# A planned order with new lengths for the vector engines' operations, a lock between two of them, and the last tile's copy in two halves

## The chip, the core and the metric

The kernel runs on one core of a Trainium2 chip. The metric is the device time of one execution in microseconds (us). PE is TensorE with its matmuls, PEld its weight loads, DVE is VectorE, ACT is ScalarE, POOL is GpSimd and SP is SyncE, which here only issues DMAs.

## What is computed

Eight batches of eight heads, each with 512 local and 32 global tokens of 64 values. The local queries see the global keys and a band of local keys, the global queries see all keys. Then every token (512 values over the heads) goes through a feed-forward layer of width 2048.

```python
def _attn_ref(q_l, k_l, v_l, q_g, k_g, v_g):
    ...
    window = 32
    scale = 1.0 / np.sqrt(D)
    k_all = np.concatenate([k_g, k_l], axis=2)
    v_all = np.concatenate([v_g, v_l], axis=2)
    s_g = scale * np.matmul(q_g, k_all.transpose(0, 1, 3, 2))
    out_g = np.matmul(sm(s_g), v_all)
    s_ll = scale * np.matmul(q_l, k_l.transpose(0, 1, 3, 2))
    pos = np.arange(Sl)
    mask = np.abs(pos[:, None] - pos[None, :]) <= window
    s_ll = np.where(mask, s_ll, -1000000000.0)
    s_lg = scale * np.matmul(q_l, k_g.transpose(0, 1, 3, 2))
    s_l = np.concatenate([s_lg, s_ll], axis=-1)
    a_l = sm(s_l)
    out_l = np.matmul(a_l, np.concatenate([v_g, v_l], axis=2))
    return np.concatenate([out_g, out_l], axis=2).astype(np.float32)

def _moe_ref(x, w_in, w_out):
    h = x @ w_in
    g = h - np.tanh(h)
    return (g @ w_out).astype(np.float32)
```

All inputs and the output are 32-bit floats; `sm` is a softmax over the last axis.

## The kernel before

**Precision.** Each operand of the feed-forward layer is split into a high part (rounded to the matmul's 32-bit type, fp32r) and a low part (the rest), and each product is made as three matmuls: high by high, low by high, high by low. So a chunk of tokens has, beside its matmuls, a cast for the high part and a subtract for the low part of everything that is made on the chip.

**Stages.** The attention of the first pairs of heads uses plain 128 x 128 transposes on PE (L547, L1176), scores L656, peak L1104 and reciprocals (L671, L672) on DVE, exponentials L1111 on ACT and the normalization L1117 on POOL, which writes `prob` or `t`; the products are L814. Later pairs use DVE's 32 x 32 stream transposes (L697, L709, L1152), band scores L730, peak L1132 (DVE), exponential L1137 (ACT), inverse L1141 and L1142 (DVE), normalization L1146 (POOL) and products L830. The global queries have scores L1030 (first pairs) and L972 (later, in halves), and turns of their probabilities L786, L788, L793, L795 on DVE. L853, L856 and L858 on DVE take the products apart into the low part of the token matrix and the sum for the global rows (`xg`).

**The feed-forward layer** runs in chunks, one for each batch of 512 local tokens (chunks of 16 steps of the hidden width, 128 columns each) and a last one for the 256 global tokens. A step is: L1219, 12 matmuls into one PSUM buffer (a `bank`) that give h; L1227, the tanh on ACT into `t`; L1230, t = h - tanh(h) on DVE; a cast of `t` to the high part of `gates` (L364, the copy helper's line, on ACT); L1236, `gates`' low part as a subtract; and L1282, which multiplies the gates by `w_out` into four accumulators (12 matmuls of 512 columns for each step). The rows of the output are copied out of PSUM (L364 `wraw<-bank`) and sent by L1312.

**Weights.** They arrive in 32 pieces beside the first 120 us or so: L418 loads a piece into `wraw` or `first_q`, L429 (ACT), L433 and L438 (DVE) bring it to the form `sq`, L364 casts the high part (`w_in_hi`, `w_out_hi`), and L444 makes the low part, on POOL or DVE.

**What sets the order.** `Order` is a list planner that runs when the program is built. Every operation is given to it by `add(engine and length, function, due, ...)` with its reads, writes, reserved names and PSUM buffers. The planner simulates five engines (T for PE, A, D, P, S) with these lengths and takes, again and again, the operation that can start first, with `KD * due` added to the start; where two engines are possible (`either`, `subtract`) each has a penalty out of the table `CFG`. A due time is made of the step and an offset of that table. An operation with `lock=True` on DVE, and each one on POOL, holds a common line "L", so that the plan never lets the two overlap. `filler` (L1509) puts up to six dummy matmuls on PE where the plan shows it a gap of over 0.6 us in the first 72 us. The instructions then stand on each engine's queue in the plan's order, and each waits at its queue's head until what it needs is done.

## Time and profile before

| | |
|---|---|
| median of three runs | 911.08 us (910.80 to 911.83) |
| the profiled execution | 911.43 us |
| its span, first to last instruction | 909.5 us |
| mean granted clock of PE, as a share | 0.995 |
| busy PE / DVE / ACT / POOL | 893.2 / 499.2 / 363.5 / 347.4 us |
| gates' subtract L1236, all 136 on POOL | 175.3 us |
| L1230 on DVE, 136 | 93.6 us |
| copies `wraw<-bank` 128x512: DVE 21, ACT 13 | 13.9 and 7.2 us |

The span is the time between the first and the last instruction of the profiled execution; the execution itself is 1.9 us longer. Times in the trace are counted from the span's start. A matmul's busy time is modelled at its end, since matmuls are pipelined: a group of L1282 shows 0.39 us each, while they follow each other more closely. An entry of the timeline may join several instructions of one line (its count is the x at its end), and the bracket gives the time in which the engine stood still before it and the operation that released it.

### The profile page before, as it was taken

The numbers are of one execution on the slowest core, as the hardware profiler recorded it, in microseconds if no ns is written. First come the engines' busy times: TensorE is split into PE (matmuls) and PEld (weight loads), VectorE is DVE, ScalarE is ACT, GpSimd is POOL, SyncE is SP. The second block draws the span as 40 slices with busy tenths as digits, with TensorE's granted clock in tenths as the row PEclk, the third lists the DMA queues.
The fourth block names the chain that finished last, engine by engine and source line by source line (L and its number), as shares of the span: only waits on it lengthen the run. The fifth ranks groups of instructions, "written<-read, shape, count | busy, mean of one in ns | idle before, by whom it ended". The sixth has DMA issues, their size and how long they took to land.

```text
span 909.5 us, 23414 instructions
## 1 busy us (share of the span) xinstructions
PE 893.2 (98%) x9101; PEld 719.4 (79%) x9101; DVE 499.2 (55%) x1829; ACT 363.5 (40%) x1024; POOL 347.4 (38%) x506
## 2 busy tenths in 40 slices
PE   8999899999999999999999999999999999999998
PEld 5678678788878878788878788787888788888896
DVE  6898878836648364746557374746566461211211
ACT  5886555523334343333344343433333331222221
POOL 5576675423333333333334333333333331222221
PEclk9999999999999999999999999999999999999999
DMA  9776674755546344645545443644555321100100
GB/s 203 189 189 184 189 185 110 181 117 115 119 97 163 79 99 103 157 111 120 120 117 142 100 100 87 161 105 110 117 137 133 94 66 30 47 1 1 45 2 23
DMA packets 286958, 101.13 MB, mean 111 GB/s; under 512 B 254848, under 2 KB 277376, under 8 KB 286848
## 3 DMA queue, kind: packets, MB, share of 16 engines
q1 hardware_dynamic: 284800, 98.53, 44.4%
q8 instruction: 71, 1.16, 0.5%
q10 hardware_dynamic: 2048, 1.11, 0.4%
q14 instruction: 39, 0.32, 0.1%
HBM read 76.01 MB, written 21.50 MB: 107 GB/s over the span
## 4 chain that ended last, share of the span: by engine, by line
PE 88%; DVE 5%; DMA 2%; ACT 1%; SPq 1%; POOL 1%; issue 1%; ACTq 0%; DVEq 0%
PE bank L1219 39%; PE bank L1282 39%; PE bank L830 4%; PE bank L730 3%; DVE sq L438 1%; PE bank L814 1%; PE bank L972 1%; DMA first_q<-in_moe_w_out_dram 1%; PE bank L656 1%; PE bank L1030 1%; SPq L686 1%; DMA raw<-in_q_l_dram 0%; DMA wraw<-in_moe_w_in_dram 0%; DMA turned<-in_v_l_dram 0%; DVE t L1230 0%
## 5 line engine op out<-in xcount | busy, mean ns | idle before, releaser
L1236 POOL TENSOR_TENSOR gates<-t,gates 128x512 fp32r<-128x512 f32 x136 | 175.3, 1289 | 390.4 <-PE bank L1282 294.1
L1282 PE MATMUL bank<-w_out_hi,gates 128*128 128x512 f32 x1088 | 296.8, 392 | 2.4 <-ACT gates L364 1.5
L1282 PEld LDWEIGHTS bank<-w_out_hi,gates 128*128 128x128 f32 x1088 | 202.7, 188 | 47.1 <-ACT gates L364 2.2
L1230 DVE TENSOR_TENSOR t<-bank,t 128x512 f32<-128x512 f32 x136 | 93.6, 689 | 234.9 <-ACT t L1227 233.8
L1227 ACT ACTIVATE t<-bank 128x512 f32<-128x512 f32 x136 | 81.2, 597 | 273.2 <-PE bank L1219 270.0
L1282 PE MATMUL bank<-w_out_lo,gates 128*128 128x512 f32 x544 | 150.7, 391 | 0.0
L364 ACT CAST gates<-t 128x512 fp32r<-128x512 f32 x136 | 84.2, 619 | 133.6 <-PE bank L1282 83.6
L1219 PE MATMUL bank<-x_hi,w_in_hi 128*128 128x512 f32 x432 | 124.6, 404 | 0.0
L1282 PEld LDWEIGHTS bank<-w_out_lo,gates 128*128 128x128 f32 x544 | 102.0, 188 | 21.7 <-issue 0.2
L1219 PE MATMUL bank<-x_lo,w_in_hi 128*128 128x512 f32 x432 | 118.9, 391 | 0.0
L1219 PE MATMUL bank<-x_hi,w_in_lo 128*128 128x512 f32 x432 | 118.4, 390 | 0.0
L1146 POOL TENSOR_SCALAR prob<-prob,stats 128x128 f32<-128x128 f32 x224 | 82.8, 387 | 57.1 <-DVE stats L1142 56.6
L1137 ACT ACTIVATE prob<-prob,stats 128x128 f32<-128x128 f32 x224 | 86.9, 390 | 34.2 <-DVE stats L1132 34.2
L1219 PEld LDWEIGHTS bank<-x_lo,w_in_hi 128*128 128x128 f32 x432 | 81.4, 189 | 17.9 <-issue 0.2
L1219 PEld LDWEIGHTS bank<-x_hi,w_in_lo 128*128 128x128 f32 x432 | 81.0, 188 | 17.8
L1219 PEld LDWEIGHTS bank<-x_hi,w_in_hi 128*128 128x128 f32 x432 | 78.0, 189 | 20.5 <-issue 4.0
L793 DVE STREAM_TRANSPOSE turned<-pg 32x96 f32<-32x96 f32 x288 | 77.7, 270 | 4.3
L1132 DVE CUSTOM_DVE_ANT_0 prob<-bank,band 128x128 f32<-128x128 f32 x224 | 50.6, 283 | 38.4 <-PE bank L730 37.8
L1152 DVE STREAM_TRANSPOSE sq<-prob 128x512 f32<-128x512 f32 x50 | 35.3, 710 | 13.3 <-POOL prob L1146 11.6
L1137 ACT ACTIVATION_READ_ACCUMULATOR prob<-prob,stats 128x1 f32 x224 | 42.1, 188 | 0.0
L830 PEld LDWEIGHTS bank<-turned 128*32 128x32 f32 x3072 | 33.1, 111 | 8.5 <-DVE stats L1142 6.7
L853 DVE TENSOR_TENSOR x_lo<-bank,x_hi 128x256 fp32r<-128x256 f32 x56 | 23.4, 419 | 29.1 <-ACT x_hi L364 26.6
(161 smaller groups left out, 916.7 us busy)
## 6 DMA issues: line engine op xcount, KB each, us to landing
moved<-sq SPq DMA_DIRECT2D x24, 512.0 KB, 3.9
turned<-in_v_l_dram SPq DMA_DIRECT2D x23, 512.0 KB, 5.5
turned<-in_v_l_dram SPq DMA_DIRECT2D x32, 256.0 KB, 3.2
out_dram<-wraw SPq DMA_DIRECT2D x32, 256.0 KB, 2.4
rawkq<-in_q_l_dram SPq DMA_DIRECT2D x112, 64.0 KB, 2.3
rawkq<-in_k_l_dram SPq DMA_DIRECT2D x112, 64.0 KB, 2.3
turned<-moved SPq DMA_DIRECT2D x48, 128.0 KB, 2.7
turned<-moved SPq DMA_DIRECT2D x96, 64.0 KB, 2.3
```

What stands on the lines that cost most here:

```text
L364: (nc.scalar.copy if e == "A" else eng[e].tensor_copy)(dst, src)
L793: nc.vector.transpose(win_g[G * g:G * g + G, a.two, 3 * x:3 * x + 3], view(pgh[r, a.two, G * (j + x):G * (j + x) + 1], [(3 * G, 3), (1, G)]))
L830: m = nc.tensor.matmul(y, win_v[:, NW * a.two + w, G * d:G * d + G], x, start=n == 0, stop=n == 7, skip_group_check=True)
L1132: nc.vector.tensor_tensor_reduce(out=x[:, t], in0=self.scores[:, t], in1=bands[0 if t == 0 else 2 if t == NT - 1 else 1], scale=-0.125, sc ...
L1137: nc.scalar.activation(x[:, t], x[:, t], AF.Exp, bias=self.st[:, t:t + 1], scale=-1.0, accum_out=self.st[:, 4 + t:5 + t])
L1146: nc.gpsimd.tensor_scalar(x[:, t], x[:, t], self.st[:, 8 + t:9 + t], 1.0, op0=ALU.mult, op1=ALU.mult)
L1152: nc.vector.transpose(z[:, :, self.two].rearrange("p n t c -> p t n c"), x[:, :, k * n * G:(k + 1) * n * G].rearrange("p t (n c) -> p t n ...
L1219: nc.tensor.matmul(self.h[s][:, j * n:(j + 1) * n], w[:, cc, f * P:(f + 1) * P], self.x()[xi](cc)[:, :n], start=part == 0 and cc == 0 and ...
L1227: nc.scalar.activation(tt_[q], self.h[s], AF.Tanh)
L1230: nc.vector.tensor_sub(tt_[q], self.h.pop(s), tt_[q])
L1236: eng[e].tensor_sub(gg[q][1], tt_[q].rearrange("p (k c) -> p k c", k=4), f32(gg[q][0]))
L1282: nc.tensor.matmul(self.acc[tt], g[:, j * nt + tt], low_out(f) if wi else w_out_hi[:, f], start=s == 0 and k == 1, stop=last and k == 3 * ...
```

## The change

The table `CFG` of offsets and penalties is new from end to end. Lengths in the calls of `add` are set anew, mostly by some hundredths of a microsecond, some by up to half a microsecond. The two operations `inverse` of the local pairs (the reciprocals of L672, and L1141 with L1142) get `lock=True`, so that the plan keeps them apart from POOL's. The copies of global keys cost less on POOL in the plan. And the last row tile of the last chunk is copied in two halves, one by DVE and one by ACT; its DMAs wait for both. Lines behind L1315 are 10 later in the changed kernel, those from L1509 on 11.

```diff
-    CFG = dict(a_g=-0.566, a_kg=24.4216, a_ph=0.3207, a_qs=43.4596, a_w=-0.4573, a_wn=-0.6947, a_xg=108.5443, d_g=87.2943, d_kg=23.5203,
...
+    CFG = dict(a_g=-2.1233, a_kg=-0.0964, a_ph=-0.2641, a_qs=5.2608, a_w=-5.4882, a_wn=-5.0581, a_xg=150, d_g=3.6283, d_kg=1.9778, d_ph=50.4226,
...
-        p = [("P", 0.17 + n * 0.00192, CFG["p_" + kind])] if "p_" + kind in CFG else []
+        p = [("P", 0.17 + n * (0.0009 if kind == "kg" else 0.00192), CFG["p_" + kind])] if "p_" + kind in CFG else []
...
-            add(("A", 0.655), rebias, due, r=keys, w=keys + [("up", u)])
-            add(("D", 0.42), low, due, r=keys, w=keys, lock=True)
+            add(("A", 0.67), rebias, due, r=keys, w=keys + [("up", u)])
+            add(("D", 0.48), low, due, r=keys, w=keys, lock=True)
...
-            add(("D", 0.37), inverse, n[0][1] - 0.5, r=[x[3] for x in n], w=[x[2] for x in n])
+            add(("D", 0.37), inverse, n[0][1] - 0.5, r=[x[3] for x in n], w=[x[2] for x in n], lock=True)
...
-                add(("D", 1.35 if self.j >= OWN else 1.75), turn, self.due(self.C["o_tg"]), r=["pg0"], w=[f"hg{a.two}"])
+                add(("D", 1.65 if self.j >= OWN else 1.6), turn, self.due(self.C["o_tg"]), r=["pg0"], w=[f"hg{a.two}"])
...
-            add(("D", 1.5), peak, due(1), r=[sg, ("mask", 1), "of"], w=all_ + [st], free=[(sg, 1), (sh, 1)])
-            add(("A", 0.95), exp, due(1.5), r=[st], w=all_)
-            add(("D", 0.65), inverse, due(2), r=["pg0"], w=[st])
-            add(("P", 1.45), norm, due(2.5), r=[st], w=all_)
+            add(("D", 2.05), peak, due(1), r=[sg, ("mask", 1), "of"], w=all_ + [st], free=[(sg, 1), (sh, 1)])
+            add(("A", 1.15), exp, due(1.5), r=[st], w=all_)
+            add(("D", 1.1), inverse, due(2), r=["pg0"], w=[st])
+            add(("P", 1.25), norm, due(2.5), r=[st], w=all_)
...
-            add(("D", 1.16), peak, d(1), r=[s] + [("band", j) for j in range(3)], w=[p, st], free=[(s, 1)])
-            add(("A", 1.6), exp, d(1.5), r=[st], w=[p])
-            add(("D", 0.33), inverse, d(2), r=[p], w=[st])
-            add(("P", 1.5), norm, d(2.5), r=[st], w=[p])
+            add(("D", 0.95), peak, d(1), r=[s] + [("band", j) for j in range(3)], w=[p, st], free=[(s, 1)])
+            add(("A", 1.64), exp, d(1.5), r=[st], w=[p])
+            add(("D", 0.38), inverse, d(2), r=[p], w=[st], lock=True)
+            add(("P", 1.45), norm, d(2.5), r=[st], w=[p])
...
-                    add(either(512, "y", True), out_copy, due + 0.5, r=[acc], w=[key], free=[(acc, 1)])
+                    if self.final and tt == nt - 1:
+                        def half(lo):
+                            def fn(e, _, tt=tt, key=key):
+                                copy(e, wraw[key[1]][:, lo:lo + DM // 2], self.acc[tt][:, lo:lo + DM // 2])
+                            return fn
+
+                        add(("D", 0.42), half(DM // 2), due + 0.5, r=[acc], w=[key + ("b",)], res=[key], free=[(acc, 2)])
+                        add(("A", 0.37), half(0), due + 0.5, r=[acc], w=[key], free=[(acc, 2)])
+                    else:
+                        add(either(512, "y", True), out_copy, due + 0.5, r=[acc], w=[key], free=[(acc, 1)])
...
-                    add(("S", 0.6 * k), out_dma(runs[:k]), due + 0.5, r=[key], w=[("out", self.name, tt)], xfer=0.78)
+                    parts = [key, key + ("b",)] if self.final and tt == nt - 1 else [key]
+                    add(("S", 0.45 * k), out_dma(runs[:k]), due + 0.5, r=parts, w=[("out", self.name, tt)], xfer=0.78)
...
+    chunks[-1].final = True
```

**What it does to the instructions.** On PE the matmuls are the same in number but for the dummies, 13 before and 21 now. Of the 136 subtracts L1236, DVE had none and now has 101; POOL had all and now has 35. Of the 32 subtracts L444, DVE had none and now has nine. The copies `wraw<-bank` were 21 on DVE and 13 on ACT; now DVE has the one half, and ACT all others. Thirty copies of global keys go from POOL to ACT, six copies of a bank into the first keys from DVE to ACT, and four casts of `xg` from ACT to DVE. In the steady state PE changes between its kinds of work as often as before (27 groups of L730, 24 of L830, 12 of L972).

DVE's queue at the first gates of the feed-forward layer (`t_66` and `t_67` are the two buffers for the tanh, `bank_` numbers are PSUM buffers); before:

```order
L433 TENSOR_SCALAR first_q<-first_q 128x512
L438 SCALAR_TENSOR_TENSOR sq<-first_q 128x512
L1230 TENSOR_TENSOR t_67<-bank_103,t_67 128x512
L1152 STREAM_TRANSPOSE x_hi1b<-prob_92 128x4x2x32
L1152 STREAM_TRANSPOSE x_lo1b<-prob_92 128x4x2x32
L1141 TENSOR_SCALAR stats<-stats 128x4
L1142 RECIPROCAL stats<-stats 128x4
L1230 TENSOR_TENSOR t_66<-bank_105,t_66 128x512
```

and now:

```order
L444 TENSOR_TENSOR w_in_lo<-sq,w_in_hi 128x4x128
L433 TENSOR_SCALAR first_q<-first_q 128x512
L438 SCALAR_TENSOR_TENSOR sq<-first_q 128x512
L1230 TENSOR_TENSOR t_67<-bank_102,t_67 128x512
L1230 TENSOR_TENSOR t_66<-bank_103,t_66 128x512
L697 STREAM_TRANSPOSE kw<-rawkq 128x8x64
```

The transposes L1152 now stand further ahead, L1141 and L1142 further behind, and the two L1230 follow each other; a subtract L444 has come to DVE just ahead.

PE's queue around the products L814 that stood at 99 us (`bank_98` to `bank_101` are the four buffers that the hidden steps and the attention share); before:

```order
L1219 MATMUL bank_99<-x_hi_75,w_in_hi 128x512 x4
L1219 MATMUL bank_99<-x_lo_76,w_in_hi 128x512 x4
L1219 MATMUL bank_99<-x_hi_75,w_in_lo 128x512 x4
L1219 MATMUL bank_100<-x_hi_75,w_in_hi 128x512 x4
L1219 MATMUL bank_100<-x_lo_76,w_in_hi 128x512 x4
L1219 MATMUL bank_100<-x_hi_75,w_in_lo 128x512 x4
L814 MATMUL bank_98<-turned 64x160 x4
L814 MATMUL bank_98<-turned 64x128 x4
L814 MATMUL bank_99<-turned 64x160 x4
L814 MATMUL bank_99<-turned 64x128 x2
L814 MATMUL bank_99<-turned 64x160 x2
```

and now:

```order
L1219 MATMUL bank_98<-x_hi_75,w_in_hi 128x512 x4
L1219 MATMUL bank_98<-x_lo_76,w_in_hi 128x512 x4
L1219 MATMUL bank_98<-x_hi_75,w_in_lo 128x512 x4
L814 MATMUL bank_99<-turned 64x160 x4
L814 MATMUL bank_99<-turned 64x128 x4
L814 MATMUL bank_100<-turned 64x160 x4
L814 MATMUL bank_100<-turned 64x128 x2
L814 MATMUL bank_100<-turned 64x160 x2
L1219 MATMUL bank_101<-x_hi_75,w_in_hi 128x512 x4
L1219 MATMUL bank_101<-x_lo_76,w_in_hi 128x512 x4
L1219 MATMUL bank_101<-x_hi_75,w_in_lo 128x512 x4
```

The products take other buffers, `bank_99` and `bank_100` in place of `bank_98` and `bank_99`, and one of the two groups of L1219 ahead of them now stands behind them.

ACT's queue at the end of the program (`bank_104` and `bank_105` are accumulators of the last chunk's two row tiles, `wraw_64` the buffers for the output); before:

```order
L1227 ACTIVATE t_67<-bank_100 128x512
L364 CAST gates<-t_67 128x4x128
L1227 ACTIVATE t_66<-bank_98 128x512
L364 CAST gates<-t_66 128x4x128
L1312 DMA out_dram<-wraw_64 32x512 x4
L1541 UNCONDITIONAL_BRANCH
```

and now:

```order
L1227 ACTIVATE t_66<-bank_101 128x512
L364 CAST gates<-t_66 128x4x128
L364 COPY wraw_64<-bank_105 128x512
L1312 DMA out_dram<-wraw_64 32x512 x2
L364 COPY wraw_64<-bank_104 128x256
L1312 DMA out_dram<-wraw_64 32x512 x2
L1552 UNCONDITIONAL_BRANCH
```

Before, both copies stood on DVE and ACT had the four DMAs alone; now ACT copies the first tile, issues two DMAs, copies its half of the second and issues the other two, while DVE's last row is the other half.

## Rows read from the trace of the kernel before

**Rows 1.** The page's first part: busy us, share of the span, instructions.

```profile
PE 893.2 (98%) x9101; PEld 719.4 (79%) x9101; DVE 499.2 (55%) x1829; ACT 363.5 (40%) x1024; POOL 347.4 (38%) x506
```

**Rows 2.** Busy us (instructions) of PE, PEld, DVE, ACT, POOL; clock, DMA share, GB/s.

```profile
0.00:25.00 25.00, 20.61 (x115) 14.12 (x117) 16.16 (x78) 15.36 (x47) 14.29 (x36) 0.93 0.93 217
...
75.00:100.00 25.00, 23.45 (x120) 19.19 (x121) 19.67 (x48) 14.40 (x31) 16.91 (x16) 1.00 0.70 183
...
100.00:125.00 25.00, 23.00 (x162) 17.42 (x159) 21.95 (x65) 15.28 (x39) 17.68 (x22) 0.93 0.65 184
...
875.00:900.00 25.00, 25.00 (x157) 22.49 (x156) 3.46 (x5) 5.78 (x10) 5.17 (x4) 1.00 0.00 1
```

**Rows 3.** Timeline of PE: start, busy, line, names, count [idle before <-releaser].

```profile
14.94 0.97 PE L1176 MATMUL bank<-idr,prob 128*128 128x128 f32 x4 [0.63 <-POOL prob L1117]
...
41.41 0.44 PE L1176 MATMUL bank<-idr,t 128*128 128x128 f32 x2 [0.15 <-POOL t L1117]
```

**Rows 4.** Timeline, all engines, at the first gates.

```profile
61.01 1.28 POOL L444 TENSOR_TENSOR w_out_lo<-sq,w_out_hi 128x512 fp32r<-128x512 f32 x1
...
61.16 0.59 ACT L1227 ACTIVATE t<-bank 128x512 f32<-128x512 f32 x1
...
61.20 1.12 DVE L1141 TENSOR_SCALAR stats<-stats 128x4 f32<-128x4 f32 x1
...
61.30 0.97 PE L1282 MATMUL bank<-w_out_hi,gates 128*128 128x512 f32 x3 [0.69 <-ACT gates L364]
...
63.16 0.50 PE L1282 MATMUL bank<-w_out_hi,gates 128*128 128x512 f32 x1 [0.89 <-DVE t L1230]
```

**Rows 5.** Timeline, all engines, around 99 us.

```profile
98.68 0.69 DVE L1230 TENSOR_TENSOR t<-bank,t 128x512 f32<-128x512 f32 x1 [1.18 <-ACT t L1227]
...
99.42 0.98 PE L814 MATMUL bank<-turned 128*64 128x160 f32 x12 [1.55 <-DVE t L1230]
```

**Rows 6.** Timeline around 106 us, then the clock of three stretches, columns as in 2.

```profile
105.88 1.28 DVE L433 TENSOR_SCALAR first_q<-first_q 128x512 int32<-128x512 int32 x1
...
108.70 1.58 PE L730 MATMUL bank<-kw,hi 64*32 64x128 f32 x62 [2.00 <-DVE xg L856]
...
108.70:110.00 1.30, 1.30 (x62) 1.12 (x62) 1.26 (x7) 1.05 (x2) 1.28 (x2) 0.69 0.78 170
...
110.00:112.00 2.00, 2.00 (x15) 1.49 (x5) 1.80 (x11) 1.36 (x7) 1.24 (x2) 0.50 0.64 223
...
112.00:113.00 1.00, 1.00 (x4) 0.76 (x3) 1.00 (x8) 0.85 (x4) 0.00 (x0) 0.69 0.03 4
```

**Rows 7.** Timeline around 175 us, of two windows.

```profile
171.83 1.68 DVE L793 STREAM_TRANSPOSE turned<-pg 32x96 f32<-32x96 f32 x6
...
175.15 0.73 PE L1282 MATMUL bank<-w_out_hi,gates 128*128 128x512 f32 x2 [0.79 <-ACT gates L364]
```

**Rows 8.** Groups of instructions: names, shapes xcount | busy us, mean ns | idle before.

```profile
L1236 POOL TENSOR_TENSOR gates<-t,gates 128x512 fp32r<-128x512 f32 x136 | 175.3, 1289 | 390.4 <-PE bank L1282 294.1
...
L1230 DVE TENSOR_TENSOR t<-bank,t 128x512 f32<-128x512 f32 x136 | 93.6, 689 | 234.9 <-ACT t L1227 233.8
...
L1132 DVE CUSTOM_DVE_ANT_0 prob<-bank,band 128x128 f32<-128x128 f32 x224 | 50.6, 283 | 38.4 <-PE bank L730 37.8
...
L1141 DVE TENSOR_SCALAR stats<-stats 128x4 f32<-128x4 f32 x56 | 13.2, 235 | 4.4 <-ACT prob L1137 4.4
...
L364 ACT COPY wraw<-bank 128x512 f32<-128x512 f32 x13 | 7.2, 584 | 4.3 <-DMA out_dram<-wraw 2.7 <-PE bank L1282 1.6
```

**Rows 9.** Timeline of the last matmuls, the last copy and ACT's issues.

```profile
904.78 0.40 PE L1282 MATMUL bank<-w_out_lo,gates 128*128 128x512 f32 x1
...
904.79 2.23 ACTq L1312 DMA_DIRECT2D out_dram<-wraw  x4
...
905.02 0.39 PE L1282 MATMUL bank<-w_out_hi,gates 128*128 128x512 f32 x1
...
905.44 0.69 DVE L364 COPY wraw<-bank 128x512 f32<-128x512 f32 x1 [0.68 <-PE bank L1282]
```

More of the change, by code (lines that the diff above doesn't have):

```diff
@@ L596, in add_transpose @@
             add(("T", 0.42), mm, due, r=[f"pg{u}"], w=[tg], res=["hg0", "hg1"], alloc=[(tg, self.tag)], rows=0.5, mode=1)
-            add([("A", 0.6, 0.0), ("D", 0.65, CFG.get("d_tg", PEN))], store, due + 0.3, r=[tg], w=["hg0", "hg1"], free=[(tg, 1)])
+            add([("A", 0.48, 0.0), ("D", 0.65, CFG.get("d_tg", PEN))], store, due + 0.3, r=[tg], w=["hg0", "hg1"], free=[(tg, 1)])
         def add_values(self):
@@ L872, in add_products @@
                 add(either(256, "ph", True), high(p), due + 0.5, r=[o[p]], w=[k + (0,) for k in x[p]])
-                add(("D", 0.55 if new else 0.65), rest(p), due + 1, r=[o[p]] + [k + (0,) for k in x[p]], w=[k + (1,) for k in x[p]] + xg_, free=[(o[p], 1)])
+                add(("D", 0.55 if new else 0.73), rest(p), due + 1, r=[o[p]] + [k + (0,) for k in x[p]], w=[k + (1,) for k in x[p]] + xg_, free=[(o[p], 1)])
     def add_globals(b):
```

32 lines of the change are left out of this document (16 added, 16 removed).

## The prediction

> **What bounds the kernel now.** I read the busy times first. PE works 893.2 of the 909.5 us of the span [rows 1], so a change of order can take away no more than the 16.3 us in which PE stands still, plus what the clock loses. Next the stretches of 25 us: PE is busy 20.61 in the first, 23.45 in the fourth, 23.00 in the fifth and 25.00 of 25 in one near the end [rows 2]; behind 175.15 us no entry of PE's timeline carries an idle time. So all that this change can win lies in the first 175 us and in the tail; the 730 us between can only lose. Then those entries, from left to right.
>
> The start: seven waits for POOL's normalized probabilities (L1117, L1050), the first of 0.63 and the last of 0.15, together 4.13 us [rows 3].
>
> The first gates: L1282, which needs the gates of the FFN's first two steps, waits 0.69 for ACT's cast and then 0.89 for the second L1230 (DVE, h - tanh h) [rows 4]. Ahead of that L1230 stood L1141, an operation on 4 columns, for 1.12 us beside a POOL subtract (L444) of 1.28; over the kernel L1141 takes 0.235 in the mean [rows 4, 8].
>
> At 99.42 a product L814 waits 1.55 for an L1230 that began only at 98.68 [rows 5]. At 108.70 the band scores L730 wait 2.00 for L856, which stood on DVE behind the weight operation L433 of 1.28 [rows 6]. After it the granted clock is 0.69, 0.50 (1.2 of 2.4 GHz) and 0.69 for 1.30, 2.00 and 1.00 us [rows 6]: 0.31 x 1.30 + 0.50 x 2.00 + 0.31 x 1.00 = 1.71 us lost, while it is 1.00 in the fourth stretch [rows 2]. At 175.15 L1282 waits 0.79 for a cast whose L1230 stood behind groups of six L793, 1.68 us each [rows 7].
>
> The tail: the last matmul starts at 905.02, 0.24 after the one before it, and the last tile's copy takes 0.69 from 905.44 [rows 9].
>
> **The change part by part.** The new durations and the lock enter only the plan; no instruction gets cheaper by them. PE has the same matmuls in both orders but for the dummies (13 before, 21 after), so I cost the places.
>
> First gates. In the new order DVE's two L1230 stand back to back and L1141 behind them, and ACT runs both L1227 before the first cast. So the 0.89 is gone, the first cast may come up to one L1227 (0.59) later [rows 4], partly inside the dummies ahead of it: I take -0.7. Ends: -1.58 (both waits gone) and 0.
>
> At 99 us. Before, L814 took two buffers, one of which an L1219 had filled 24 matmuls earlier and which waited for its L1230. Now it takes two that are long free, and an L1219 group stands on each side. The 1.55 goes, unless L814's other operands are late. Ends: -1.55 and 0.
>
> At 106 us. Before, 24 L1282 stood between L814 and the L730 that reuses its buffer, at 0.24 each [rows 9] 5.8 us of cover, in which DVE lost 1.28 to one operation. Now 12 L1219, 20 L1282, 12 L1219 and 4 L1282 come before the next user of those buffers, 48 x 0.24 = 11.5 us. The 2.00 goes and the clock's 1.71 with it. Ends: -3.71 and 0.
>
> At 175 us. Two groups of six L793 still stand ahead of the L1230. Ends: -0.79 and 0.
>
> Together 0.7 + 1.55 + 3.71 + 0.79 = 6.75 us if all goes (7.63 by the ends). What is late next? The weight pieces are prepared up to about 115 us, each with an L433 and an L438 that exclude POOL's work; between 100 and 125 us DVE is busy 21.95 and POOL 17.68 of 25 us [rows 2]. One blocked operation at a queue's head was enough for each of the waits above, and where one goes the queue behind it shows the next. I let half come back elsewhere, for want of a row that says which: **-3.4**, ends 0 and -7.6.
>
> The gates' subtract. 101 of the 136 L1236 move from POOL to DVE. A subtract of this size takes 1.289 on POOL; on DVE the nearest row is L1230 with 0.689 [rows 8]: 70 us on an engine that is busy 499 of 909 [rows 1]. The step's chain (L1227, L1230, cast, L1236) comes to 0.59 + 0.69 + 0.6 + 0.69 = 2.6 us with the cast at about the ACT copy's time [rows 4, 8], and PE has 48 matmuls or so between a step's last L1219 and its first L1282 in the steady state, 11.5 us. I cost it at nothing. That cover fails only where DVE's queue is late, which is rival (d).
>
> L1236 has both operands in SBUF, and the rows show that a DVE operation beside POOL's can be stretched: L1141 by 0.9 us [rows 4, 8]. The Trainium skill (SBUF — State Buffer, Who interferes with whom) has a rule that speaks against this move: a DVE instruction with two SBUF inputs and a GpSimd instruction that reads SBUF share a pair of ports, one of the two waits until the other is done, and a DVE instruction with one SBUF input (L1230, whose other input is in PSUM) doesn't. By it each moved L1236 can be late by what POOL runs at the time; no row of this trace has L1236 on DVE.
>
> The start. Six copies of bank into the first keys and four of first_g move to ACT, and DVE has two transposes and two L444 more but six copies less ahead of its first L1230. ACT's six, at 0.584 at most [rows 8], are 3.5 us if each lies on the path; the eight more dummies (8 x 0.24 = 1.9 us) lie inside such waits. On the other side half of the 4.13 us of POOL's waits may go, since POOL gives up copies and subtracts: -2.1. That the new plan has more gaps that draw dummies speaks for the later end: I take **+0.5**, ends -2.1 and +3.5.
>
> The tail. Before, ACT's four issues lie in 904.79 to 907.02 [rows 9], two of them after the copy's end at 906.13, so 0.45 each. Now ACT copies the first tile (0.584 [rows 8], to about 904.7), issues two and then copies its half: start 905.6, 0.29 to 0.58 long, end 905.9 to 906.2 in place of 906.13. **-0.1**, ends -0.25 and +0.1.
>
> Sum: -3.4 + 0.5 - 0.1 = -3.0. The profiled execution took 911.43, which is 0.35 over the median of 911.08: the sum gives 908.4 on it and 908.1 on the median.
>
> **The rivals.**
> (a) All late waits go and the start keeps its time: -6.75 - 0.1, **904.2**. For it: each of the three large waits hangs on one place in two queues, and the new order changes each. Against: the same three engines feed the same stretch.
> (b) The start gets later by ACT's copies and eats the gain: -3.4 + 3.5 - 0.1, **911.1**. For it: 21 dummies in place of 13. Against: POOL, for which PE waited there, gets lighter.
> (c) The order doesn't matter here: the weights' arrival and blocked operations set the stretch from 60 to 125 us whatever stands where, **911.0**. For it: DVE's 21.95 of 25 us [rows 2]. Against: the buffers of L814 really differ.
> (d) Slower, by new waits in the gapless part. In the new order the global halves' scores L972 follow 12 L1282 after the L730 whose buffers they take, at five sites: 12 x 0.24 = 2.9 us. In that time DVE must do eight L1132, 50.6/224 = 0.226 each [rows 8], and an L1230: 1.8 + 0.69 = 2.5. With an L1236 among them it is 3.2; with that one held up by a POOL operation of 1.29 [rows 8] it is 4.5, and PE waits 1.6. Five sites are 8.0 us, 908.1 + 8.0 = **916.1**. Four make it slower by more than a measurement's bound (908.1 + 6.4 = 914.5), two only take the gain. For it: there is no slack once an L1236 stands between, and the rule above, by which it comes out so where POOL is at work. Against: POOL, busy 347 of 909 us with the subtracts [rows 1], has lost most of them.
>
> **How the numbers follow.** Forecast (half of the waits) 0.38, (a) 0.23, (b) 0.15, (c) 0.09, (d) 0.15. A measurement of this kernel can tell about 0.2%, 1.8 us, from no change: faster is below 909.3, slower above 912.9. The forecast's own spread is some 2 us to each side, so 0.33 of its 0.38 are faster; with (a) and the milder 0.06 of (b), 0.62. Same: 0.05 of the forecast, 0.08 of (b) and (c), 0.22. Slower: (d) and the rest of (b), 0.16. The range leaves out the start's gain on top of (a), and most of (d): 904.0 to 912.5.
>
> **What would show it.** Right: no idle entry of PE over 1 us between 63 us and the tail, a granted clock of 1.00 from 100 to 125 us, the second L1230 of the first gates 0.7 after the first, L814 and L730 near 100 us with no DVE releaser, and 101 L1236 on DVE near 0.69 each. Rival (a): PE's idle times from 63 to 176 us add to less than 1 us. Rival (b): the first L1282 later than 61.30 by 2 us or more. Rival (c): they still add to 4 or more. Rival (d): L972 or L730 idle behind 175 us with DVE as releaser, and L1236 on DVE well over 0.69 in the mean. The forecast is wrong in kind if PE idles in the part that was gapless.

## The result: 6 us slower

| | before | changed |
|---|---|---|
| median | 911.28 us | 917.39 us |
| lowest to highest of four | 910.80 to 911.83 | 915.89 to 919.13 |
| the profiled execution / its span | 911.43 / 909.5 us | 916.99 / 915.2 us |
| start of the first L1282 | 61.30 | 63.46 |
| from there to the end of the span | 848.2 us | 851.7 us |
| idle entries of PE: up to 60 us / from there to 180 us / behind | 5.81 / 5.92 / 0 us | 6.51 / 4.68 / 3.87 us |
| L1219 behind the same matmuls | 176.19 | 175.93 |
| L1282 behind the same matmuls, near 234 us | 233.99 | 233.78 |
| L1282 behind the same matmuls, near 900 us | 896.98 | 902.52 |
| last matmul's start to the end, by the unrounded spans | 4.53 us | 4.65 us |

The ratio is 1.0068 with the interval 1.0048 to 1.0087. 917.4 lies beyond the range (904.0 to 912.5) and on the other side. (The 6.51 holds a wait of 1.75 us at 57.78, which belongs to the first gates.)

"Behind the same matmuls" means: counted line by line and without the dummies, PE has by then done the same matmuls in both kernels. So the two starts can be compared, though the orders differ. The lines near 234 and 900 us, first of the kernel before, then of the changed one:

```profile
233.99 1.07 PE L1282 MATMUL bank<-w_out_hi,gates 128*128 128x512 f32 x4
...
896.98 1.09 PE L1282 MATMUL bank<-w_out_hi,gates 128*128 128x512 f32 x4
```

```profile
233.78 1.07 PE L1282 MATMUL bank<-w_out_hi,gates 128*128 128x512 f32 x4
...
902.52 1.09 PE L1282 MATMUL bank<-w_out_hi,gates 128*128 128x512 f32 x4
```

The changed kernel is 2.2 us later at the first L1282, level again at 176 us and at 234, and 5.5 later near 900 us. So its loss lies behind 234 us: 668.74 us in place of 662.99, which is 5.75 more. The time in front of it varies from execution to execution: four profiled executions of this same order (this one and three of the runs below) start that L1219 at 175.33 to 177.64.

The page of the changed kernel, in the order of [rows 1] and [rows 8]: busy times and three groups.

```profile
span 915.2 us, 23456 instructions
...
PE 895.0 (98%) x9109; PEld 720.6 (79%) x9109; DVE 550.6 (60%) x1916; ACT 386.2 (42%) x1078; POOL 204.3 (22%) x366
...
L1230 DVE TENSOR_TENSOR t<-bank,t 128x512 f32<-128x512 f32 x136 | 92.9, 684 | 173.1 <-ACT t L1227 172.7
...
L1236 DVE TENSOR_TENSOR gates<-t,gates 128x512 fp32r<-128x512 f32 x101 | 70.5, 698 | 100.0 <-PE bank L1282 91.2
...
L1236 POOL TENSOR_TENSOR gates<-t,gates 128x512 fp32r<-128x512 f32 x35 | 46.1, 1319 | 47.2 <-PE bank L1282 25.7
```

PE is busy 1.8 us longer, which is the length of the eight more dummies: 12 L1282 follow one another in 2.72 us (228.33 to 231.05), 0.2265 each. DVE is up by 51 us, POOL down by 143. The moved L1236 take 698 ns each on DVE, near L1230's 684.

The first gates, timeline of ACT, PE and DVE, and then an entry of SP's queue (answer to [rows 4]):

```profile
56.80 0.67 ACT L429 ACTIVATE wraw<-wraw 128x512 f32<-128x512 f32 x1 [1.68 <-DMA wraw<-in_moe_w_in_dram]
...
57.78 0.49 PE L1245 MATMUL bank<-x_hi,w_in_hi 128*128 128x512 f32 x1 [1.75 <-ACT x_hi L364]
...
59.67 0.62 ACT L364 CAST w_in_hi<-sq 128x512 fp32r<-128x512 f32 x1 [0.40 <-DVE sq L438]
...
60.20 0.67 ACT L429 ACTIVATE first_q<-first_q 128x512 f32<-128x512 f32 x1
...
60.78 1.05 ACT L1227 ACTIVATE t<-bank 128x512 f32<-128x512 f32 x2
...
62.07 1.28 DVE L1230 TENSOR_TENSOR t<-bank,t 128x512 f32<-128x512 f32 x2
...
63.46 1.30 PE L1282 MATMUL bank<-w_out_hi,gates 128*128 128x512 f32 x4 [2.43 <-ACT gates L364]
...
52.16 0.43 SPq L418 DMA_DIRECT2D wraw<-in_moe_w_in_dram  x1
```

The two L1230 run back to back (1.28 for both), L1141 is gone from between them, and the wait of 0.89 with it. But all of it stands later. On ACT an L429 stood 1.68 at the queue's head for a piece of w_in, whose load L418 was issued at 52.16 between two sets of raw loads L686 (49.06 and 52.69), and the cast of x_hi behind it made PE wait 1.75. Then ACT runs a cast and an L429 of weight pieces before the two L1227, and L1282 waits 2.43: 4.18 in the place of 1.58.

The stretch behind it, by windows (columns as in [rows 2]), and two of the five waits from 64 to 176 us that stand where 1.55, 2.00 and 0.79 stood ([rows 5 to 7]):

```profile
64.00:66.00 2.00, 2.00 (x7) 1.52 (x6) 1.74 (x6) 1.94 (x7) 2.00 (x3) 0.61 0.79 247
...
66.00:68.00 2.00, 2.00 (x7) 1.56 (x6) 1.96 (x4) 0.70 (x4) 0.84 (x1) 0.54 0.59 89
...
100.00:125.00 25.00, 24.65 (x168) 19.05 (x168) 19.82 (x61) 15.90 (x40) 17.32 (x20) 1.00 0.64 176
```

```profile
92.30 2.23 PE L814 MATMUL bank<-turned 128*64 128x160 f32 x30 [0.59 <-DVE turned L786]
...
165.83 1.70 PE L814 MATMUL bank<-turned 96*64 96x128 f32 x24 [0.66 <-DMA turned<-sq]
```

The five waits add to 0.59 + 0.35 + 0.40 + 0.25 + 0.66 = 2.25 us in place of 4.34. The clock is whole between 100 and 125 us; but behind the waits at the first gates it loses 0.39 x 2 + 0.46 x 2 = 1.70 us between 64 and 68, as much as behind the wait at 108.70 before. From the first L1282 to the L1219 at 176 us it is 114.9 us before and 112.5 now: the smaller waits win back what the first gates lost.

Behind 176 us, where the kernel before had no idle entry, PE waits at 11 places, always an L830 for the last L795 of the turn. One of them, with DVE's and POOL's queues ahead of it:

```profile
225.71 0.42 DVE L982 CUSTOM_DVE_ANT_0 pg<-bank,mask 128x256 f32<-128x256 f32 x1
...
226.87 0.68 DVE L977 COPY stats<-stats 32x2 f32<-32x2 f32 x4
...
228.96 1.37 DVE L977 COPY stats<-stats 32x2 f32<-32x2 f32 x4
...
231.36 1.30 DVE L1152 STREAM_TRANSPOSE sq<-prob 128x512 f32<-128x512 f32 x2
...
232.58 0.60 DVE L895 STREAM_TRANSPOSE qgt<-qgt 64x128 f32<-64x128 f32 x2
...
235.12 1.68 DVE L793 STREAM_TRANSPOSE turned<-pg 32x96 f32<-32x96 f32 x6
...
236.82 0.20 DVE L795 STREAM_TRANSPOSE turned<-pg 32x32 f32<-32x32 f32 x1
...
228.20 2.80 POOL L1146 TENSOR_SCALAR prob<-prob,stats 128x128 f32<-128x128 f32 x8 [21.21 <-DVE stats L1141]
...
231.03 1.00 POOL L1003 TENSOR_SCALAR pg<-pg,stats 128x288 f32<-128x288 f32 x2
...
237.07 1.56 PE L830 MATMUL bank<-turned 128*32 128x64 f32 x128 [0.42 <-DVE turned L795]
```

DVE has no gap from the peak L982 at 225.71 to the end of the turn at 237.02: 11.3 us. PE has 48 matmuls of L1219 and L1282 between L972 and this L830, 48 x 0.2265 = 10.9 us (48 or 44 at the other places). In the kernel before it has 72 (56 at one place), and the turn's last L795 ends 2.5 to 8.8 us ahead of each of these L830. The plan's lengths for the halves' inverse (1.1) and the turn (1.65) are short of what stands here: 1.37 for four L977 and 0.47 more for L997 and L998, and 1.68 + 0.20.

The end of the program (answer to [rows 9]):

```profile
910.56 0.39 PE L1282 MATMUL bank<-w_out_hi,gates 128*128 128x512 f32 x1
...
910.99 0.42 DVE L364 COPY wraw<-bank 128x256 f32<-128x256 f32 x1 [4.74 <-PE bank L1282]
...
911.45 0.37 ACT L364 COPY wraw<-bank 128x256 f32<-128x256 f32 x1 [1.25 <-DVE wraw L364]
```

By the profile ACT's half was released by DVE's half: the halves run one behind the other and end 1.26 after the last matmul's start; the whole copy ended 1.11 after it.

### The profile page after: what moved, and what is told of

The parts are those of the page before. It is cut to its first block, busy times and chain, and to the rows that moved or that the text cites. A ratio compares the mean times of both kernels' runs of the same rounds, so it can differ in the third digit from the quotient of the medians.

```text
span 915.2 us, 23456 instructions
## 1 busy us (share of the span) xinstructions
PE 895.0 (98%) x9109; PEld 720.6 (79%) x9109; DVE 550.6 (60%) x1916; ACT 386.2 (42%) x1078; POOL 204.3 (22%) x366
## 3 DMA queue, kind: packets, MB, share of 16 engines
q10 hardware_dynamic: 2048, 1.11, 0.5%
## 4 chain that ended last, share of the span: by engine, by line
PE 74%; DVE 16%; ACT 4%; DMA 2%; SPq 2%; issue 2%; POOL 0%; ACTq 0%; DVEq 0%; POOLq 0%
PE bank L1282 33%; PE bank L1219 31%; DVE turned L793 4%; PE bank L830 4%; PE bank L730 3%; DVE stats L977 2%; DVE t L1230 2%; SPq L752 1%; DVE sq L1152 1%; PE bank L972 1%; DVE sq L438 1%; DVE pg L982 1%; PE bank L1245 1%; ACT turned L364 1%; DVE turned L795 1%
## 5 line engine op out<-in xcount | busy, mean ns | idle before, releaser
L1282 PE MATMUL bank<-w_out_hi,gates 128*128 128x512 f32 x1088 | 299.3, 395 | 2.8 <-ACT gates L364 2.8
L1282 PEld LDWEIGHTS bank<-w_out_hi,gates 128*128 128x128 f32 x1088 | 200.8, 188 | 50.8 <-issue 5.0
L1230 DVE TENSOR_TENSOR t<-bank,t 128x512 f32<-128x512 f32 x136 | 92.9, 684 | 173.1 <-ACT t L1227 172.7
L1146 POOL TENSOR_SCALAR prob<-prob,stats 128x128 f32<-128x128 f32 x224 | 91.1, 425 | 457.6 <-DVE stats L1142 264.0
L1227 ACT ACTIVATE t<-bank 128x512 f32<-128x512 f32 x136 | 80.8, 596 | 234.1 <-PE bank L1219 233.7
L1282 PE MATMUL bank<-w_out_lo,gates 128*128 128x512 f32 x544 | 151.7, 393 | 0.1
L1236 DVE TENSOR_TENSOR gates<-t,gates 128x512 fp32r<-128x512 f32 x101 | 70.5, 698 | 100.0 <-PE bank L1282 91.2
L1219 PE MATMUL bank<-x_hi,w_in_hi 128*128 128x512 f32 x432 | 120.5, 395 | 0.0
L1282 PEld LDWEIGHTS bank<-w_out_lo,gates 128*128 128x128 f32 x544 | 102.5, 188 | 22.4 <-issue 0.3
L1219 PE MATMUL bank<-x_hi,w_in_lo 128*128 128x512 f32 x432 | 118.6, 390 | 0.0
L1219 PE MATMUL bank<-x_lo,w_in_hi 128*128 128x512 f32 x432 | 118.3, 390 | 0.0
L1219 PEld LDWEIGHTS bank<-x_lo,w_in_hi 128*128 128x128 f32 x432 | 81.0, 188 | 17.3 <-issue 0.2
L1219 PEld LDWEIGHTS bank<-x_hi,w_in_lo 128*128 128x128 f32 x432 | 80.6, 188 | 17.6 <-issue 0.2
L1219 PEld LDWEIGHTS bank<-x_hi,w_in_hi 128*128 128x128 f32 x432 | 79.6, 188 | 17.6 <-issue 0.6
L793 DVE STREAM_TRANSPOSE turned<-pg 32x96 f32<-32x96 f32 x288 | 77.5, 269 | 5.6
L1236 POOL TENSOR_TENSOR gates<-t,gates 128x512 fp32r<-128x512 f32 x35 | 46.1, 1319 | 47.2 <-PE bank L1282 25.7
L1152 DVE STREAM_TRANSPOSE sq<-prob 128x512 f32<-128x512 f32 x50 | 34.6, 703 | 33.5 <-POOL prob L1146 32.1
L830 PEld LDWEIGHTS bank<-turned 128*32 128x32 f32 x3072 | 33.4, 111 | 13.1 <-DVE turned L795 8.5
```

The lines of the kernel that those rows point to most:

```text
L793: nc.vector.transpose(win_g[G * g:G * g + G, a.two, 3 * x:3 * x + 3], view(pgh[r, a.two, G * (j + x):G * (j + x) + 1], [(3 * G, 3), (1, G)]))
L830: m = nc.tensor.matmul(y, win_v[:, NW * a.two + w, G * d:G * d + G], x, start=n == 0, stop=n == 7, skip_group_check=True)
L1146: nc.gpsimd.tensor_scalar(x[:, t], x[:, t], self.st[:, 8 + t:9 + t], 1.0, op0=ALU.mult, op1=ALU.mult)
L1152: nc.vector.transpose(z[:, :, self.two].rearrange("p n t c -> p t n c"), x[:, :, k * n * G:(k + 1) * n * G].rearrange("p t (n c) -> p t n ...
L1219: nc.tensor.matmul(self.h[s][:, j * n:(j + 1) * n], w[:, cc, f * P:(f + 1) * P], self.x()[xi](cc)[:, :n], start=part == 0 and cc == 0 and ...
L1227: nc.scalar.activation(tt_[q], self.h[s], AF.Tanh)
```

## The experiments

In most of them the plan is made as it stands and single operations are then moved in the finished list, past operations on which they don't depend; everything else keeps its place. The kernel before measured 910.8 to 911.6 beside each of them.

### The turn and L830

```diff
+    for j in range(10, 32, 2):
+        i = next(i for i, v in enumerate(out) if _name(v).endswith("mm_windows") and ("o0", "pair", j) in v[2].args)
+        k = next(k for k in range(i + 1, len(out)) if out[k][3] == "T")
+        _hoist(out, k, i)
```

> The changed kernel with its order kept, but at the 11 places from 237 to 745 us where L830 waited for the turn L795 (0.20 to 0.57 us each, 3.87 together), the L1219 or L1282 group behind L830 (4 matmuls, 0.9 us) is put ahead of it. Theory A (the loss is these waits): they vanish, and at 0.05 to 0.1 more than the idle time for each, 4.5 to 5.5 us go: 917.4 becomes 912 to 913. Theory B (the loss is in the first 175 us, where the first gates wait 1.75 and 2.43): the time stays above 915. Theory C (DVE is too full): the waits come back at the next place where PE needs DVE.

Measured 914.70 (ratio to the kernel before 1.0035, 1.0022 to 1.0048). The 11 waits are gone, as theory A says, though 914.70 is later than its 912 to 913; one wait of 0.54 at 650 us is new.

```diff
...
+        for k in turns:                      # the two turns of the pair, behind the norm
+            _hoist(out, k, at)
+            at += 1
```

> The changed kernel, with DVE's queue alone altered: at the same 11 places the turn (L793, L795) stands directly behind the normalization's place in the plan, ahead of one or two L1152 (0.65 each) and L895 (0.60). Theory A1 (the turn is late for what stands ahead of it on DVE): at 237 us it can start at 232.03, when POOL's L1003 ends, in place of 233.22, so the waits vanish and 912 to 913 comes out as in the first run. Theory A2 (POOL's norm sets it): the waits shrink by less than half, 915 or more.

Measured 913.70 (1.0031, 1.0018 to 1.0045). The place at 237 us, timeline:

```profile
236.07 0.20 DVE L795 STREAM_TRANSPOSE turned<-pg 32x32 f32<-32x32 f32 x1
...
237.11 1.57 PE L830 MATMUL bank<-turned 128*32 128x64 f32 x128
```

The turn ends 0.84 us ahead of L830 (0.1 at places with 44 matmuls), with the same matmuls in between as in the changed kernel; one wait of 0.57 at 649 us is new. Of the 6.1 us, 2.7 to 3.7 go with the waits, less than expected. In the profiled executions the stretch from the L1282 near 234 us to that near 900 us takes 664.26 and 664.39 us in these two runs, 668.74 in the changed kernel and 662.99 in the kernel before: the 11 waits cost 4.4 of the 5.75 us, more than their 3.87 of idle time, and 1.3 to 1.4 are left, about 1 of them around the new wait. A1 holds, A2 falls.

```diff
...
+        if v[0] > 180 and v[3] == "D" and _name(v).endswith("Chunk.add_hidden.rest"):
+            out[i] = (*v[:3], "P")
```

> The changed kernel with its order kept, but from 180 us on all gates' subtracts L1236 (98) go back from DVE to POOL, at their places in the order. Theory C (the moved subtracts fill DVE): near 225 us an L1236 waited 0.43 for PE and took 0.69 just ahead of the peak L982; without it the turn is up to 1.1 us earlier and the 11 waits of L830 vanish: 912 to 913. Theory A (the place of L830 in the order alone): the waits stay, 916 to 918.

Measured 919.04 (1.0093, 1.0076 to 1.0111): the waits didn't vanish, they grew to 6.84 us in 11 entries.

```profile
231.62 1.29 POOL L1236 TENSOR_TENSOR gates<-t,gates 128x512 fp32r<-128x512 f32 x1 [0.23 <-ACT gates L364]
...
234.63 1.77 DVE L793 STREAM_TRANSPOSE turned<-pg 32x96 f32<-32x96 f32 x6
...
236.69 1.56 PE L830 MATMUL bank<-turned 128*32 128x64 f32 x128 [0.65 <-DVE turned L795]
```

A POOL subtract of 1.29 now lies beside the turn, and six L793 take 1.77 in place of 1.68. From 234 to 900 us it takes 671.05, which is 2.3 us more than the changed kernel. So theory C falls: the moved subtracts don't make the waits, and in this order they are a gain.

```diff
...
+        if v[0] > 180 and v[3] == "P" and _name(v).endswith("Chunk.add_hidden.rest"):
+            out[i] = (*v[:3], "D")
```

> The kernel before, its order kept, but all gates' subtracts L1236 from 180 us on are made by DVE in place of POOL, at the same places in the order. The prediction's step (the move costs nothing in the steady state, since PE has 40 matmuls and more between a step's L1219 and its L1282): 911 within 1 us, and no idle entry of PE behind 180 us. Rival by the port rule (an L1236 on DVE is held up by POOL's norms): L1236 well over 0.69 in the mean, and PE waits: 913 or more.

Measured 911.60 (1.0010, 1.0000 to 1.0021), and no idle entry behind 180 us; from 234 to 900 us it takes 663.17, 0.2 more than the kernel before. The group of DVE's subtracts:

```profile
L1236 DVE TENSOR_TENSOR gates<-t,gates 128x512 fp32r<-128x512 f32 x116 | 80.1, 690 | 88.5 <-PE bank L1282 71.4 <-ACT gates L364 15.1 <-ACT turned L364 1.4
```

### Offsets and lengths

`g1_offsets_only` is the kernel before with the new table, `g2_lengths_only` the changed kernel with the old table.

> The kernel before with the new table of offsets alone (old lengths, no lock, old tail). In its order 40 matmuls of L1219 and L1282 stand between the scores L972 and the L830 that needs their turn; in the changed kernel it is 44 or 48, in the kernel before 72. 40 x 0.2265 = 9.1 us against the 11.3 us that DVE needed from the peak L982 to the end of the turn (225.7 to 237.0 in the changed kernel). Theory A (the offsets put L830 too near): waits of about 2 us at each of 10 or 11 places, 20 us and more: 930 or later. Theory D (the new lengths or the lock did it): no such waits, 909 to 913.

Measured 944.20 (1.0364). The first of these waits:

```profile
243.09 2.57 PE L830 MATMUL bank<-turned 128*32 128x64 f32 x128 [2.74 <-DVE turned L795]
```

11 such entries, 0.64 to 2.98 each and 18.9 us together, about as expected from 40 matmuls. The first L1282 starts at 69.59, which is 8.3 us more.

> The changed kernel with the old table of offsets (new lengths, lock and tail). 72 matmuls between L972 and L830, as in the kernel before. Theory A: no waits of L830 for the turn; the time is that of the kernel before but for the first 175 us and the tail, 909 to 913. Theory D: L830 waits and 914 or more.

Measured 933.87 (1.0251). No L830 waits for its turn: that half of theory A holds. From 234 to 900 us it takes 663.12, as in the kernel before. The time was missed by 20 us, because the start falls apart with these lengths and the old offsets (the first L1282 starts at 78.41); the longest wait in front of it:

```profile
55.22 0.80 PE L587 MATMUL bank<-idr,pg 64*128 64x64 f32 x5 [4.46 <-POOL pg L1050]
```

So the two halves of the change belong together; neither table is good with the other's lengths. The short distance from L972 to L830 comes with the new table.

```diff
-                add(("D", 1.65 if self.j >= OWN else 1.6), turn, self.due(self.C["o_tg"]), r=["pg0"], w=[f"hg{a.two}"])
+                add(("D", 1.9 if self.j >= OWN else 1.9), turn, self.due(self.C["o_tg"]), r=["pg0"], w=[f"hg{a.two}"])
...
-            add(("D", 1.1), inverse, due(2), r=["pg0"], w=[st])
+            add(("D", 1.85), inverse, due(2), r=["pg0"], w=[st])
```

> The changed kernel with two lengths of the plan set to what the trace of it shows: the turn 1.9 (in place of 1.65 and 1.6; 1.68 + 0.20 measured) and the inverse of the global halves 1.85 (in place of 1.1; 1.37 + 0.30 + 0.17 measured). The plan is made anew: between L972 and L830 stand 48 and 52 matmuls by turns, in place of 48 and 44. Theory A (the plan left no slack since these lengths were short): the waits of 0.25 at the places that had 44 go, those of 0.42 at the places with 48 stay, 2 us in all; the time is 914 to 917, unless the new plan of the start moves it.

Measured 915.42 (1.0040, 1.0026 to 1.0054). All 11 waits are gone, not half of them: one more group of 4 matmuls at half of the places and what DVE was given to do elsewhere was enough. From 234 to 900 us it takes 663.42, 0.4 more than the kernel before: with these two lengths the plan loses next to nothing there. The new plan of the start gave 2.66 back at one place:

```profile
166.08 2.31 PE L814 MATMUL bank<-turned 128*64 128x160 f32 x14 [2.66 <-DVE stats L998]
```

### The stretch from 60 to 180 us

```diff
+    at = _find(out, 395)                     # L814 at 99 us
+    for s in (484, 485):                     # two groups of L1282
+        _hoist(out, _find(out, s), at)
+        at += 1
+    at = _find(out, 500)                     # L730 at 106 us
+    for s in (541, 542):                     # two groups of L1219
+        _hoist(out, _find(out, s), at)
+        at += 1
```

> The kernel before, with its order kept but for PE: at 99 us eight L1282 go ahead of the L814 that waited 1.55, at 106 us eight L1219 go ahead of the L730 that waited 2.00. If the prices of these two waits in the prediction hold (1.55 + 2.00 + 1.71 of clock = 5.26), the time is 911.1 - 5.3 = 905.8; if the waits only move to the next place, 909 to 911.

Measured 911.49 (1.0001, 0.9991 to 1.0010). The wait at 99 us is gone, the one at 108.6 is not, and one has come at 136:

```profile
108.56 1.74 PE L730 MATMUL bank<-kw,hi 64*32 64x128 f32 x55 [1.91 <-DVE xg L856]
...
136.37 1.14 PE L730 MATMUL bank<-hl,hi 64*32 64x128 f32 x62 [1.77 <-DVE t L1230]
```

```diff
+    _hoist(out, _find(out, 397), _find(out, 360))        # L853, L858, L856 ahead of L433
+    _hoist(out, _find(out, 638), _find(out, 554))        # L1230 ahead of L438
+    _hoist(out, _find(out, 346), _find(out, 345) + 1)    # the second L1230 of the first gates
```

> The kernel before with the two moves on PE of the earlier run (eight L1282 ahead of the L814 at 99 us, eight L1219 ahead of the L730 at 106 us), which left the time at 911.5 since the wait at 108.6 stayed at 1.91 and one of 1.77 came at 136, and now with three moves on DVE: L853, L858 and L856 go ahead of the L433 and L438 that stood before them at 105.9, the L1230 of 135.6 goes ahead of an L438 of 1.74, and the second L1230 of the first gates goes ahead of L1141 and L1142. Theory A (one blocked operation at the head of DVE's queue makes each wait): the waits at 99, 106, 136 go (5.2 us with the clock) and the 0.9 at 63 shrinks: 905.5 to 907. Theory B (the stretch is full, so a wait comes back wherever PE gets ahead): 909.5 to 911.5, with new waits of 1 to 2 us between 100 and 180 us.

Measured 910.38 (0.9990, 0.9982 to 0.9999): the fastest of all kernels that compute the reference, by 0.9 us. All four waits that were aimed at are gone or small, and these two are new, beside one of 0.56:

```profile
110.40 1.16 PE L1219 MATMUL bank<-x_hi,w_in_hi 128*128 128x512 f32 x4 [1.78 <-DVE stats L1132]
...
146.90 1.34 PE L814 MATMUL bank<-turned 128*64 128x160 f32 x18 [1.49 <-DVE turned L786]
```

The idle entries from 63 to 180 us add to 5.23 in the kernel before, 5.33 in the first of these two and 4.70 in the second. Theory B holds for these moves.

```diff
+    _sink(out, _find(out, 413), _find(out, 191))     # raw loads behind weight loads, SP
+    _sink(out, _find(out, 414), _find(out, 185))
+    _hoist(out, _find(out, 255), _find(out, 192))    # cast of x_hi ahead of L429, ACT
```

> The second run's kernel (turn first, 913.7) and three moves at the first gates: on SP's queue two sets of raw loads (L686, 3.00 and 2.36 us of issuing) go behind the weight loads L418 that stood behind them, and on ACT's queue a cast of x_hi goes ahead of the L429 that waited 1.68 for its weight piece. Theory A (what is left of the loss is that the first gates come 2.2 us later, because the weight piece is loaded later): the first L1282 comes near 61.3 in place of 63.3, and the time falls by about 2, to 911.5 to 912. Theory E (waits between 63 and 180 us take it back, as when the waits at 99 us of the kernel before were moved): 913 to 914.

Measured 913.49 (1.0029, 1.0014 to 1.0043): L1245 waits 0.35, the first L1282 starts at 62.28 after 2.42 of waiting, and the median is 0.2 less than with the turn first alone. The time is theory E's, but the first L1282 came forward by half of what theory A asks for, so A isn't refuted by it.

> The changed kernel with the turn first (as in the second run), the start's moves (as in the run of the start), and three more at the first gates, where ACT's two L1227 stood 1.1 us behind the cast and the L429 of a weight piece: L1227 twice ahead of that cast, the two L1230 ahead of DVE's L444, the casts of the gates ahead of the w_out cast. The last tile's copy is whole again, on ACT. Theory A (what is left over the kernel before, 2.2 us, is that the first L1282 starts at 63.3 in place of 61.3): the first L1282 starts near 60.8 and the rest of the run keeps its 848.1 us, so the span is 909.0, the time 911. Theory E (later waits take it back): the first L1282 is earlier, the rest longer by as much, 912.5 to 913.5. The tail: in the kernel before the span ends 4.48 after the last matmul's start, with the split copy 4.64; if the two halves ran one behind the other, the whole copy gives 4.5 again.

Its edit puts L1227, L1230 and the casts of the gates ahead of the weight piece's steps in the same way. Measured 914.80 (1.0032, 1.0021 to 1.0044). Timeline of this kernel:

```profile
61.77 1.20 PE L1282 MATMUL bank<-w_out_hi,gates 128*128 128x512 f32 x4 [0.56 <-ACT gates L364]
...
93.04 0.46 PE L814 MATMUL bank<-turned 128*64 128x160 f32 x2 [3.47 <-DMA turned<-x_lo1b]
...
69.04 0.39 SPq L418 DMA_DIRECT2D wraw<-in_moe_w_in_dram  x1
```

The wait at the first gates is 0.56 and the first L1282 starts at 61.77 in place of 63.34, but from there to the end it takes 851.6 us in place of 848.1: 3.47 at 93 us and 1.38 at 75.7 are new. The weight load that the changed kernel issues at 67.42 goes out at 69.04, 1.6 us later, and the transfers behind it on SP's queue, for which that L814 waits, are later by as much. The later waits take the gain back, as in theory E, and more: 914.80 lies beyond its 913.5. The span still ends 4.67 after the last matmul's start with the whole copy on ACT: the split neither wins nor costs against that, and the expected 4.5 was wrong.

> The changed kernel with its order kept and all 21 dummy matmuls left out. If the dummies lie inside waits, the time stays at 917 within 1 us unless the clock falls; if the eight more of them cost their 1.8 us, it falls to 915.5; if the granted clock falls in the start without them, it rises.

Measured 919.04 (1.0092, 1.0060 to 1.0125). The waits to 63 us rise from 6.51 to 8.04 and the granted clock falls to 0.50 from 17 to 23 us, where it was whole, and 3.4 us are lost there: the dummies lie mostly inside waits. The intervals of the two kernels overlap, so it isn't shown that the time rises; it doesn't fall.

Last, two kernels without the 32 L429 and the 32 L433, so that the weights, and with them the output, have other values:

```diff
...
+    out[:] = [v for v in out if not (_name(v).endswith("add_weights.rebias") or _name(v).endswith("add_weights.low"))]
```

(and L438 with a right shift and an "and", so that its result stays a small number).

> The kernel before, its order kept, without the 32 L429 (ACT, 0.67 each) and the 32 L433 (DVE, 0.4 to 1.28 each) that prepare the weight pieces, so the weights and with them the output have other values; all loads, L438, casts and L444 stay. Theory F (the weight pieces, each behind the one before it through two buffers, set the pace from 60 to 130 us, and PE waits somewhere in it whatever is moved): the waits at 61, 63, 99 and 109 us shrink to less than 1 us in all from 5.1, and the time falls by 4 to 6, to 905.5 to 907.5. If those waits are only a matter of the order of the queues, they stay within 1 us and so does the time.

> The changed kernel with the turn first (913.7), its order kept, without the same 64 instructions, so with other values in the weights and the output. Theory F: the waits of 1.12 and 2.41 at the first gates and of 2.7 behind them shrink to less than 2 in all, and the time falls by 4 to 6, to 908 to 910; what is left over the first run of this pair is the eight dummies and the tail. If the time stays over 912.5, the loss of the start lies elsewhere.

Measured 904.22 (0.9927, 0.9912 to 0.9942) on the kernel before and 908.67 (0.9985, 0.9970 to 1.0000) on the changed one with the turn first: 6.5 and 4.5 us less, each against the kernel before beside it. The waits of the first that are left from 60 to 180 us:

```profile
60.77 0.50 PE L1282 MATMUL bank<-w_out_hi,gates 128*128 128x512 f32 x1 [0.48 <-DVE t L1230]
...
166.75 1.20 PE L1282 MATMUL bank<-w_out_hi,gates 128*128 128x512 f32 x4 [0.88 <-ACT gates L364]
```

5.92 us have become 1.36. On the changed kernel 2.41 and 1.12 at the first gates have become one wait,

```profile
62.93 1.20 PE L1282 MATMUL bank<-w_out_hi,gates 128*128 128x512 f32 x4 [1.37 <-ACT gates L364]
```

and two of 0.40 and 0.98 are left up to 180 us. So the preparation of the weight pieces sets the pace of that stretch, and with two of its steps gone the same orders run almost without a wait; the first kernel is even faster than theory F's 905.5. Leaving out 64 operations also unloads ACT and DVE: whether the chain of the pieces through two buffers paces the stretch, as theory F has it, or the mere load of ACT and DVE, these runs don't tell.

## Why the prediction was wrong

**Where the gain could lie** was read rightly (the first 175 us, and behind them only losses), and the rival for the other side was looked for in the right part. It named the wrong pair: L972 behind L730 and an L1236 in DVE's way. L972 never waited there, and that rival (d)'s 916.1 came near the 917.4 is luck. What waited was L830 for the turn, at 11 places, and the cause was no subtract (with them on POOL the waits grew) but the distance: 72 matmuls became 48 or 44, and DVE's work from the peak to the turn, with what stands ahead of the turn in its queue, is 11.3 us. More matmuls in between, or the turn further ahead on DVE, each took the waits away. PE idles in the part that was gapless, which the prediction called wrong in kind. The step that failed is the cover in the part on the gates' subtract: I counted PE's work between L1219 and L1282 of a step and between L730 and L972 (at 0.24 us each, where 0.2265 is measured), and for the longest chain of the steady state, from L972 over peak, exponential, inverse, norm and turn to L830, I counted none, though both orders show it. Price: 4.4 us in the profiled executions from 234 to 900 us, 2.7 to 3.7 in the medians. The 851.7 against 848.2 from the first L1282 on is less, since the stretch up to 176 us won 2.4.

**First gates**: the two L1230 stand back to back, as read. The step that failed is the -0.7: it counted what stands between the gates' operations and not what stands ahead of them, and the waits that were to shrink by 0.7 grew by 2.6. With the loads and the cast of x_hi moved ahead, L1245's wait fell from 1.12 to 0.35, but L1282's stayed at 2.42; only with L1227, L1230 and the casts of the gates ahead of the weight piece's steps was it 0.56. The first L1282 is 2.16 later, which was rival (b)'s sign, but this is no second loss: at 176 us it has been won back.

**99, 106 and 175 us**: the three waits went (1.55, 2.00, 0.79), and the half that I let come back is what came back in waits (2.25 of 4.34). The clock's 1.71 went from there and came at the first gates. But at 176 us all this is worth 0.3 us in the profiled executions, in place of the 2.9 that the forecast has for this part (-3.4 + 0.5). The step that failed is to give each wait a price of its own: taking two and then four of them away in the kernel before brought 0 and 0.9 us. Rival (c), at 0.09, had the reason, and its sign: from 63 to 176 us PE's idle times add to 4.68, with the 2.43. It deserved more of the chance, and rows that spoke for it were there: DVE at 21.95 of 25 us, and an L433 of 1.28 ahead of the L856 for which PE waited.

**The moved subtracts** cost nothing in the steady state: right, shown in both orders, 0.690 and 0.698 us each. Held up by POOL they were not: 15 of the 101 lay beside an L1146 and took 0.77 at most; it was POOL's operation that took longer (last section).

**The start**: the waits up to 45 us fell by 1.05 (to 4.76), with nine dummies there in place of eight, and the dummies cost nothing by themselves. The prediction left out a fall of the clock that its rows hold, 0.93 in the first 25 us [rows 2]; the changed kernel's profile has none there. The loss isn't in this part.

**The tail**: 0.12 longer in place of 0.1 shorter. The step that failed took the two halves to run side by side.

What stays open: 1.3 us of the 5.75, and the spread. The runs of the changed order spread over 3 us and more (915.9 to 919.1; with the start's moves 911.8 to 918.1), those of the kernel before mostly over 1 to 2. A part of the latter goes with the clock: 21 executions of the kernel before with a mean granted clock of 0.996 took 910.8 us in the mean, five with 0.992 took 912.3. For the changed order no run tells why.

## What to carry to other kernels

Before a new order is trusted in a part where the matrix engine never waits, count for every chain that leaves it and comes back how much of its work stands between, in the old order and in the new, and set that against the measured work of the other engines in between, with what stands ahead of it in their queues: here 48 x 0.2265 = 10.9 us against 11.3. Compare two orders at points where the same work is done; the time from one instruction to the end can hide a gain and a loss in one number. A wait that one sees in a stretch which something else paces may have no price of its own; take that something away in a trial run and see whether the waits go. Offsets that were searched with one set of lengths can be much worse with another (here by 33 and 23 us), and in a plan without slack a length that is short becomes a wait.
